# Transposes that write pairs of tokens, and weight words whose top bits are joined by 16-bit operations

## The chip, the cores and the metric

The kernel runs on one core of a Trainium2 chip. The metric is the device time of one execution in microseconds. The core has five engines that work from queues of their own: TensorE (PE in the profile, with its weight loads as PEld), VectorE (DVE), ScalarE (ACT), GpSimd (POOL) and SyncE (SP), which here only issues DMAs. Each engine takes its instructions in order, and an instruction that waits holds up all those behind it on its engine.

## The reference, cut to what matters

```python
# attention: B=4, H=8, S=768, D=48
f = 1 / (1 + exp(-f_logit))
for t in range(S):
    state = f[:, :, t, :, None] * state + einsum('bhd,bhe->bhde', k[:, :, t], v[:, :, t])
    y[:, :, t] = einsum('bhd,bhde->bhe', q[:, :, t], state)
x = y.transpose(0, 2, 1, 3).reshape(3072, 384)
# feed-forward: w_gate, w_val 384 x 1536, w_out 1536 x 384
g = x @ w_gate
out = (g * (1 / (1 + exp(-g))) * (x @ w_val)) @ w_out
```

The state decays by a gate f for each token and dimension, so the attention is a linear recurrence; its result goes through a gated feed-forward block. The activations are float32. The weights are float64: setup multiplies float32 noise by a float64 factor, and the kernel gets each weight as two 32-bit words.

## The kernel before, in words

**Units.** The tokens of a sequence are cut into six chunks of 128 (`c` from 0 to 5). A unit is one chunk of one of the four batches; unit `u` is `4 * c + b`. Within a unit, products of the gates along the tokens (two scans on VectorE) turn the recurrence into matrix products: k is multiplied by the product of the gates behind it up to the chunk's end, q by the product up to it over that of the whole chunk, scores are `k` times `q` under a causal mask, and the state of the chunk before comes in as one more product. The generator `attention(u)` yields after each step, so that the caller can lay the steps among other work.

**Getting tokens onto the free axis.** f, k and q come with tokens on partitions, and the scans need tokens along the free axis. For chunks 0 and 1 TensorE transposes them (`transposed`). For chunks 2 to 5 (`c >= SQUARES`) VectorE does, in blocks of 32 by 32. To make this work, `load` puts token `4 * t + i` of a unit on partition `t` of a group of 32, in four runs `i`, into one "room" each for f, k and q (tiles `fsquares`, `ksquares`, `qsquares`; one buffer each). A transpose of run `i` then gives every fourth token, and `in_turn` writes them to every fourth word of a row of 128 tokens.

**The steps of a unit of chunks 2 to 5,** with their lines: sigmoid of f on ScalarE (L556), transpose of f (L565), transpose of k into `kT` (L572), scan `tail` (L576), multiply of kT by it in place (L584); for units 14 to 19 (`turned`) a transpose of kT into the tile `qT`, used as scratch, and DMAs that write it to DRAM (L591, L594), from where it is read back as `kt` (L627); scan `gate` (L598), transpose of q into `qT` (L601), multiply of qT by the gate in place (L604); scores on TensorE (L617), mask on VectorE (L631), products `y` (L652, L656, L677), copies of them on ScalarE (`yT`, L660) and ten DMAs `xT<-yT` on SyncE (L667) that put them in place for the feed-forward. The last batch of a chunk takes another way to `xT`: GpSimd clears a tile `diagonal` (L544), ScalarE fills it (L546), and `y` is one set of products (L677). `yT` and `diagonal` share one buffer (tag "x").

**Loading ahead.** `load_after(u)` issues the DMAs of the next unit's f, k and q, four each, on SyncE. In chunks 2 to 5 it stands right behind L601. Since each room has one buffer, the f load waits for the end of L565, the k load for L572 and the q load for L601.

**The feed-forward** of a chunk takes all four batches at once (512 tokens). Chunk 0 is done plainly. Chunks 1 to 5 use a scheme with fifteen products in place of eighteen for the first two matrices (L957) and seven in place of eight for the third (`down_seven`: `one`, `six`, `two`, `three`, `four`, `five`, `seven`; L1056 and L1119). It costs VectorE and ScalarE additions and copies of the parts (L858, L861, L909, L962, L973). `two` ends with a copy on ScalarE of the bank "B" (L1082), of which there is one; `four` writes that bank next.

**Weights.** Each piece is fetched with its two words interleaved. ScalarE makes `up`, the low word times 2^-29 rounded to an integer, and `top`, the absolute value of the high word read as float32 (L461, L463: `sizes`). VectorE then clamps `top` (L469), shifts it left by three (L471), puts the top two bits of the high word above it (L473) and adds `up` as integers (L475): `join`. The last is named CUSTOM_DVE in the profile.

**Order.** For the start (up to about 45 us) and again from about 135 us on the order on each engine is written out: `in_order` ties every instruction to the one before it. In the latter stretch the order comes from a table of due times (`CHAINS`, `SCORES`, `times`), by which the steps of the units are laid among the products of the feed-forward. In between, while chunk 1's attention, chunk 0's feed-forward, the weights and the weights' sums run, instructions are tied only in part, and the order is the framework's.

Of the kernel before, what the change touches and what calls it, by code (L numbers as in the profile page):

```python
# [9 lines left out]
FP32 = mybir.dt.float32  # L10
I32 = mybir.dt.int32
U32 = mybir.dt.uint32
AF = mybir.ActivationFunctionType
ALU = mybir.AluOpType

# [4 lines left out]
def general_path(ctx, tc, q, k, v, f_logit, moe_w_gate, moe_w_val, moe_w_out, out):  # L20
# [70 lines left out]
    def weight_pieces(dst, src):  # L91
# [9 lines left out]
        def piece(i, j):  # L101
# [13 lines left out]
            nc.vector.tensor_scalar(man, top, 2.0 ** -20, 1.0, op0=ALU.mult, op1=ALU.add)  # L115
            nc.vector.scalar_tensor_tensor(man, lo.bitcast(U32), 2.0 ** -52, man, op0=ALU.mult, op1=ALU.add)
            nc.gpsimd.tensor_tensor(dst[:, i:i + n_a, j:j + n_n], man, p2.bitcast(FP32), ALU.mult)
# [14 lines left out]
    def attention(u):  # L132
        b, c = units[u]
        fr, qr, kr = (raw[nm][u % NRAW] for nm in "fqk")
        nc.scalar.activation(fr[:, :, 0:D], fr[:, :, 0:D], AF.Sigmoid)

# [108 lines left out]
    def mlp(g):  # L245
        h = {}

        def hidden(j):
# [5 lines left out]
            sg = ffn.tile([128, TB], FP32, tag="silu", name="silu", bufs=3)  # L254
            nc.scalar.activation(sg, gp, AF.Silu)
            h[j] = ffn.tile([128, TB], FP32, tag="h", name="h", bufs=16)
# [33 lines left out]
def short_path(ctx, tc, ident, least, judge, q, k, v, f_logit, moe_w_gate, moe_w_val, moe_w_out, out):  # L290
# [9 lines left out]
    nc = tc.nc  # L300
    B, H, S, D = q.shape
    C = 128
    NCH = S // C
    HP = H // 2
# [6 lines left out]
    N1 = C + 1  # L311
# [3 lines left out]
    SQUARES = 2  # L315
# [47 lines left out]
    def pairs(t, off=0):  # L363
        return t[:, off:off + HP * N1].rearrange("p (a t) -> p a t", t=N1)
# [30 lines left out]
    NI = C // Q  # L395
    RUN = NI * D

    rooms = {}
# [9 lines left out]
    def squares(nm):  # L408
        return rooms[nm][:, Q:Q + HP * RUN].rearrange("t (a i e) -> t a i e", a=HP, i=NI)[:, :, :, 0:Q]

    def in_turn(t):

        return t.rearrange("p a (t i) -> p a i t", i=NI)

    def load(u, what="fkqv"):
        b, c = units[u]
        rows = slice(c * C, (c + 1) * C)
        for nm, src in (("f", f_logit), ("k", k), ("q", q), ("v", v)):
            if nm not in what:
                continue  # L420
            if nm == "v":
                dst = v_of(u)
            elif c < SQUARES:
                dst = raw[nm][u % NRAW]
            else:
                for n in range(4):
                    at = Q * (1 - n % 2)
                    nc.sync.dma_start(
                        out=rooms[nm][Q * n:Q * (n + 1), at:at + HP * RUN].rearrange("t (a e) -> t a e", a=HP),
                        in_=src[b, n // 2::2, rows, :].rearrange("a (t i) d -> t a (i d)", i=NI))  # L430
                continue
            nc.sync.dma_start(out=dst[:, :, 0:D], in_=src[b, :, rows, :].rearrange("h t d -> t h d"))

    def weight_piece(dst, src, parts):

        b, a, n = dst.shape[1:]  # L440
        if src.dtype == FP32:
            by_row = src.rearrange("p a (b n) -> p a b n", n=n)
            return (lambda: [nc.sync.dma_start(out=dst[:, :, i], in_=by_row[:, i]) for i in range(a)]), [], []
        shape = [128, b // parts, a, n]
        kept = {}

        def fetch():
            kept["w"] = wst.tile([128, a, 2 * b * n], I32, tag="w64", name="w64", bufs=4)
            nc.sync.dma_start(out=kept["w"], in_=src)

        def part(m):
            return slice(m * b // parts, (m + 1) * b // parts)

        def halves(m):
            words = kept["w"].rearrange("p a (b n two) -> p a b n two", two=2, n=n)[:, :, part(m)].rearrange("p a b n two -> p b a n two")
            return words[:, :, :, :, 0], words[:, :, :, :, 1]

        def sizes(m):
            lo, hi = halves(m)
            up = wst.tile(shape, I32, tag="up", name="up", bufs=NPART)  # L460
            nc.scalar.activation(up, lo.bitcast(U32), AF.Copy, scale=2.0 ** -29)  # L461
            top = wst.tile(shape, I32, tag="top", name="top", bufs=NPART)
            nc.scalar.activation(top.bitcast(FP32), hi.bitcast(FP32), AF.Abs)  # L463
            kept["up", m], kept["top", m] = up, top

        def join(m):
            lo, hi = halves(m)
            up, top = kept["up", m], kept["top", m]
            nc.vector.tensor_scalar(top.bitcast(FP32), top.bitcast(FP32), as_float(0x38000000), as_float(0x47F00000),  # L469
                                    op0=ALU.max, op1=ALU.min)  # L470
            nc.vector.tensor_scalar(top, top, 3, 0x3FFFFFFF, op0=ALU.logical_shift_left, op1=ALU.bitwise_and)  # L471
            for i in range(b // parts):
                nc.vector.scalar_tensor_tensor(top[:, i], hi[:, i], -(1 << 30), top[:, i], op0=ALU.bitwise_and,  # L473
                                               op1=ALU.bitwise_or)
            nc.vector.tensor_tensor(dst[:, part(m)].bitcast(I32), top, up, ALU.add)  # L475

        return fetch, [lambda m=m: sizes(m) for m in range(parts)], [lambda m=m: join(m) for m in range(parts)]

    def as_float(bits):
        return struct.unpack("<f", struct.pack("<I", bits))[0]  # L480
# [31 lines left out]
    def rows_of(par):  # L512
        return slice(W * par, W * par + D)
# [3 lines left out]
    def bank(name):  # L517
        return banks[-1].tile([128, 512], FP32, tag="a", name=name)
# [3 lines left out]
    def sigmoid_ahead(u):  # L522


        fr = raw["f"][u % NRAW]
        nc.scalar.activation(fr, fr, AF.Sigmoid)
        ahead.add(u)

    def attention(u):
        b, c = units[u]  # L530
        fr, kr, qr = (raw[nm][u % NRAW] for nm in "fkq")
        v_ = v_of(u)
        gate, tail = (x[u % NROT if c < SQUARES else 0] for x in (gates, tails))

        diagonal = None

        def decay():
            nonlocal diagonal
            if c:
                nc.vector.tensor_tensor(decayed[:, :, 0:D], states[b], whole.broadcast_to((128, HP, D)), ALU.mult)  # L540
            if c and b == B - 1:

                diagonal = att.tile([128, HP, 2 * D], FP32, tag="x", name="diagonal")
                nc.gpsimd.memset(diagonal, 0.0)  # L544
                for par in range(2):
                    nc.scalar.copy(diagonal[rows_of(par), :, par * D:(par + 1) * D], decayed[rows_of(par), :, 0:D])  # L546

        def transposed(name, src):
            p = bank(name)
            for a in range(HP):  # L550
                nc.tensor.transpose(p[:, a * C:(a + 1) * C],
                                    src[:, 2 * a:2 * a + 2, :].rearrange("t r d -> t (r d)"), ident)
            return p.rearrange("p (a t) -> p a t", t=C)

        if c >= SQUARES:
            nc.scalar.activation(squares("f"), squares("f"), AF.Sigmoid)  # L556
            if b == (c > SQUARES):

                nc.scalar.activation(spare, spare, AF.Silu)
        else:  # L560
            p = transposed("fTp", fr)
# [6 lines left out]
        kT = att.tile([128, HP, C], FP32, tag="kT", name="kT")  # L568
        qT = att.tile([128, HP, C], FP32, tag="qT", name="qT", bufs=2)
        kp, qp = kT, qT  # L570
        if c >= SQUARES:
            nc.vector.transpose(in_turn(kT), squares("k"))  # L572
        yield

        n = HP * N1
        nc.vector.tensor_tensor_scan(tail[:, 0:n][:, ::-1], gate[:, 0:n][:, ::-1], floor[:, ::-1], 1.0,  # L576
                                     op0=ALU.mult, op1=ALU.max)
# [3 lines left out]
        if c < SQUARES:  # L581
            kp = transposed("kTp", kr)
            qp = transposed("qTp", qr)
        nc.vector.tensor_tensor(kT, kp, pairs(tail, 2)[:, :, 0:C], ALU.mult)  # L584
        yield
        turned = (SQUARES + 1) * B + 1 < u < (NCH - 1) * B
        if turned:
# [10 lines left out]
        nc.vector.tensor_tensor_scan(gate[:, 0:n], gate[:, 0:n], start, 1.0, op0=ALU.mult, op1=ALU.add)  # L598
        yield
        if c >= SQUARES:  # L600
            nc.vector.transpose(in_turn(qT), squares("q"))  # L601
            load_after(u)
        yield
        nc.vector.tensor_tensor(qT, qp, pairs(gate)[:, :, 1:N1], ALU.mult)  # L604
        nc.gpsimd.memset(pairs(gate)[:, :, 0:1], 0.0)
        if 0 < c < SQUARES:
            load_after(u)
        if c < SQUARES:
            decay()
# [8 lines left out]
        if c < NCH - 1 and not turned:  # L618
            p = bank("kt")
# [14 lines left out]
        if c >= SQUARES:  # L634
            decay()
# [4 lines left out]
        if c and b < B - 1:  # L640
# [20 lines left out]
            for h in range(H):  # L661
                a, par = h // 2, h % 2
                f = h * D
                while f < (h + 1) * D:
                    n = min((h + 1) * D, (f // 128 + 1) * 128) - f
# [28 lines left out]
        if c < NCH - 1:  # L694
            p = bank("dS")
# [13 lines left out]
    def load_after(u):  # L709

        w = u + (1 if units[u][1] >= SQUARES else 2)
        if w < len(units) and (units[w][1] >= SQUARES) == (w == u + 1):
            load(w, "fkqv" if units[w][1] < SQUARES or w == SQUARES * B else "fkq")
# [452 lines left out]
    mark = traced[-1]  # L1166
    keep_warm(5)
    first = [attention(b) for b in range(B)]
    done = [0] * B

# [119 lines left out]
def kernel(  # L1290
# [22 lines left out]
    def judge(bank):  # L1313
# [12 lines left out]
        yield  # L1326

    short_path(tc, ident, least, judge, *args)
    with tc.If(redo[0] > 0):
        general_path(tc, *args)  # L1330
# [32 lines left out]
```

## Time and profile before

| | us |
|---|---|
| median of three runs | 610.28 (609.24 to 611.36) |
| the profiled execution | 611.44 |
| its span, first to last instruction | 609.6 |
| TensorE busy | 595.8 |
| VectorE busy | 494.3 |
| ScalarE busy | 288.5 |
| GpSimd busy | 7.6 |

Busy time is the union of an engine's own instructions; issuing DMAs is not counted. A line of a group reads: line, engine, operation, output and inputs by name, shape, number of instructions, then their busy time, the mean time of one in ns, and the time that the engine stood idle right before them with what ended it. A line of a timeline reads: start, duration, engine, line, operation, names, shape, count, and idle time before. SPq and ACTq are DMA issues. The profile covers one execution, 1.16 us slower than the median. TensorE was granted full clock for 99.6% of the span.

### The profile page before, as it was taken

Reading aid. Unit: us, or ns where it says so; the run is one execution under the profiler, and the core shown is the slowest. Engines: PE = TensorE matmul, PEld = TensorE weight load, DVE = VectorE, ACT = ScalarE, POOL = GpSimd, SP = SyncE. Lnnn points to the kernel's source line nnn. Section 1 sums busy time; section 2 is a strip of 40 time slices with the busy share of each in tenths; the row PEclk is TensorE's granted clock in tenths of the full one; section 3 lists DMA queues with packets and bytes.
Section 4 is the critical chain, followed back from the end, with each engine's and each line's share of the span. In section 5 each row is a group of like instructions: output and inputs, shape, how many; then the busy total and the mean of one; then the engine's idle time right before and its main releaser. Section 6 shows DMA issues by size and latency. Waiting matters only on the chain.

```text
span 609.6 us, 10796 instructions
## 1 busy us (share of the span) xinstructions
PE 595.8 (98%) x4036; PEld 491.1 (81%) x4036; DVE 494.3 (81%) x833; ACT 288.5 (47%) x554; POOL 7.6 (1%) x52
## 2 busy tenths in 40 slices
PE   7899999999999999999999999999999999999996
PEld 5744545667888799888899988899988899988896
DVE  7999989868999985999996789996878981566731
ACT  3466644313776522476732366742276730366600
POOL 1000000000000000000000000000000000000000
PEclk9999999999999999999999999999999999999999
DMA  9988372005312044323236334145313100100001
GB/s 199 260 194 295 126 247 79 5 15 159 95 39 70 23 108 115 105 53 96 61 89 145 94 97 110 35 112 120 110 44 90 27 6 10 53 1 1 0 1 59
DMA packets 109142, 54.10 MB, mean 89 GB/s; under 512 B 68760, under 2 KB 102168, under 8 KB 109080
## 3 DMA queue, kind: packets, MB, share of 16 engines
q1 hardware_dynamic: 107064, 50.56, 31.3%
q10 hardware_dynamic: 2016, 2.75, 1.2%
q8 instruction: 34, 0.56, 0.4%
q14 instruction: 28, 0.23, 0.1%
HBM read 44.04 MB, written 6.29 MB: 83 GB/s over the span
## 4 chain that ended last, share of the span: by engine, by line
PE 85%; DVE 10%; SPq 1%; issue 1%; DMA 1%; ACT 1%; POOL 0%; DVEq 0%; ACTq 0%; POOLq 0%
PE o L1056 17%; PE A L957 15%; PE B L957 12%; PE gate L755 5%; PE val L755 5%; PE o L957 5%; PE c L957 5%; PE sc L617 4%; PE o L778 3%; PE o L1119 3%; PE y L677 2%; PE y L656 2%; PE dS L697 2%; PE y L652 1%; DVE c L861 1%
## 5 line engine op out<-in xcount | busy, mean ns | idle before, releaser
L1056 PE MATMUL o<-w_out,h 128*128 128x192 f32 x360 | 62.0, 327 | 0.5 <-DVE h L909 0.5
L957 PE MATMUL A<-xs,w_both 128*128 128x256 f32 x240 | 62.1, 381 | 0.0
L1056 PEld LDWEIGHTS o<-w_out,h 128*128 128x128 f32 x360 | 58.7, 190 | 1.7 <-DVE h L909 0.8
L962 ACT COPY c<-A 128x512 f32<-128x512 f32 x40 | 23.3, 583 | 62.6 <-PE A L957 62.6
L962 ACT COPY aside<-A 128x512 f32<-128x512 f32 x60 | 35.1, 584 | 32.6 <-PE A L957 32.6
L858 DVE TENSOR_TENSOR c<-c,aside 128x512 f32<-128x512 f32 x60 | 41.6, 694 | 10.5 <-ACT aside L962 9.0
L957 PEld LDWEIGHTS A<-xs,w_both 128*128 128x128 f32 x240 | 44.9, 190 | 6.5
L909 DVE TENSOR_TENSOR h<-h,c 128x256 f32<-128x256 f32 x100 | 41.1, 419 | 7.3 <-ACT h L973 7.3
L861 DVE TENSOR_TENSOR c<-c,aside 128x512 f32<-128x512 f32 x60 | 41.4, 689 | 2.5 <-ACT aside L962 2.5
L973 ACT ACTIVATE h<-c 128x256 f32<-128x256 f32 x100 | 39.2, 416 | 8.4 <-DVE c L858 5.8
L1056 PE MATMUL o<-ws,h 128*128 128x192 f32 x240 | 41.5, 328 | 0.2 <-DVE A L631 0.2
L957 PE MATMUL B<-xs,w_both 128*128 128x256 f32 x160 | 41.2, 380 | 0.6 <-ACT aside L962 0.6
L957 PE MATMUL c<-xT,w_both 128*128 128x256 f32 x160 | 41.2, 380 | 0.5 <-DVE c L861 0.5
L957 PE MATMUL A<-xs,extra 128*128 128x256 f32 x160 | 41.2, 380 | 0.0
L957 PE MATMUL B<-xT,extra 128*128 128x256 f32 x160 | 41.1, 379 | 0.0
L962 ACT COPY aside<-B 128x512 f32<-128x512 f32 x60 | 35.1, 584 | 11.7 <-PE B L957 7.2
L631 DVE TENSOR_TENSOR A<-sc,causal 128x512 f32<-128x512 f32 x48 | 30.8, 684 | 11.3 <-PE sc L617 11.3
L1056 PEld LDWEIGHTS o<-ws,h 128*128 128x128 f32 x240 | 39.1, 190 | 0.8 <-DVE A L631 0.4
L861 DVE TENSOR_TENSOR c<-o,c 128x512 f32<-128x512 f32 x40 | 27.6, 690 | 10.0 <-ACT h L973 5.8
L957 PEld LDWEIGHTS c<-xT,w_both 128*128 128x128 f32 x160 | 30.3, 190 | 5.0 <-DVE c L861 0.9
L957 PEld LDWEIGHTS B<-xs,w_both 128*128 128x128 f32 x160 | 30.2, 190 | 5.0 <-ACT aside L962 1.0
L957 PEld LDWEIGHTS A<-xs,extra 128*128 128x128 f32 x160 | 30.3, 190 | 4.5 <-ACT c L962 0.4
(138 smaller groups left out, 1140.2 us busy)
## 6 DMA issues: line engine op xcount, KB each, us to landing
fsquares<-in_f_logit_dram SPq DMA_DIRECT2D x64, 96.0 KB, 2.6
ksquares<-in_k_dram SPq DMA_DIRECT2D x64, 96.0 KB, 2.3
qsquares<-in_q_dram SPq DMA_DIRECT2D x64, 96.0 KB, 2.2
v<-in_v_dram SPq DMA_DIRECT2D x24, 192.0 KB, 3.0
w<-in_moe_w_gate_dram SPq DMA_DIRECT2D x6, 768.0 KB, 6.3
w<-in_moe_w_val_dram SPq DMA_DIRECT2D x6, 768.0 KB, 5.1
w<-in_moe_w_out_dram SPq DMA_DIRECT2D x6, 768.0 KB, 5.3
out_dram<-ob ACTq DMA_DIRECT2D x14, 192.0 KB, 2.7
```

The lines of the kernel that those rows point to most:

```text
L617: nc.tensor.matmul(sc[par][:, a * C:(a + 1) * C], lhsT=kT[r, a, :], rhs=qT[r, a, :], start=True, stop=True)
L631: nc.vector.tensor_tensor(A[:, par], sc[par].rearrange("p (a t) -> p a t", t=C), causal.unsqueeze(1).broadcast_to((128, HP, C)), ALU.mult)
L755: nc.tensor.matmul(p, lhsT=w[:, j, i, :], rhs=xT[c][:, i, :], start=(i == 0), stop=(i == KT - 1))
L778: nc.tensor.matmul(p, lhsT=hidden_tile(h, n // 2)[:, n % 2 * 2 + b // 2, b % 2 * C:(b % 2 + 1) * C], rhs=w_out[:, j, :], start=(n == 0), s ...
L858: nc.vector.tensor_tensor(dst, a, b, ALU.add)
L861: nc.vector.tensor_tensor(dst, a, b, ALU.subtract)
L909: lagging.append(lambda: f(*args))
L957: nc.tensor.matmul(p[name][:, n, :], lhsT=weights_of[a][:, n, j, :], rhs=tokens[b], start=fresh and n == 0, stop=True, skip_group_check=True)
L962: nc.scalar.copy(t, p[name])
L973: nc.scalar.activation(dst, src[:, 0, :], AF.Silu)
L1056: nc.tensor.matmul(p[:, n, :], lhsT=lhsTs[j][:, n * C:(n + 1) * C], rhs=rhs[:, j, :], start=first and j == order[0] and n == 0, stop=j == ...
L1119: nc.tensor.matmul(p, lhsT=hidden_tile(h, j)[:, 2, n * C:(n + 1) * C], rhs=b22[:, j, :], start=j == order[0], stop=j == order[-1])
```

## The change

Two edits go together.

In the weights, ScalarE writes the rounded low word only into the lower 16 bits of each word of `up`. VectorE masks the topmost 16 bits of the high word with 0xC000 and writes them into the upper 16 bits of `up`, one instruction for a join. The instructions L473 (one, or two, for a join) are gone, and the sum of `top` and `up` is as before.

In chunks 2 to 5, the transposes of k and q write two runs of tokens to every second word of one half of a row, and the other two runs to the other half (`parted`). The multiplies that follow read such a row in pairs of words, two from one half and two from the other, and write tokens in their right order (`multiply`). The two transposes therefore write scratch tiles and no longer the tiles that are multiplied in place: k goes to the tile `qT`, and q to k's room. `load_after` moves behind the multiply of q, since k's room is in use until then. The transpose of f is as before.

```diff
+        def split_squares(nm):
+            return squares(nm).rearrange("t a (j i) e -> t a j i e", j=2)
+        def parted(t):
+            return t.rearrange("p (j a t i) -> p a j i t", j=2, a=HP, i=NI // 2)
...
+        def high_ends(m):
+            quarters = kept["w"].bitcast(U16).rearrange("p a (b n four) -> p a b n four", four=4, n=n)[:, :, part(m)]
+            return quarters.rearrange("p a b n four -> p b a n four")[:, :, :, :, 3]
...
-            nc.scalar.activation(up, lo.bitcast(U32), AF.Copy, scale=2.0 ** -29)
+            ends = up.bitcast(U16).rearrange("p b a (n two) -> p b a n two", two=2)
+            nc.scalar.activation(ends[:, :, :, :, 0], lo.bitcast(U32), AF.Copy, scale=2.0 ** -29)
...
-            for i in range(b // parts):
-                nc.vector.scalar_tensor_tensor(top[:, i], hi[:, i], -(1 << 30), top[:, i], op0=ALU.bitwise_and,
-                                               op1=ALU.bitwise_or)
+            ends = up.bitcast(U16).rearrange("p b a (n two) -> p b a n two", two=2)
+            nc.vector.tensor_single_scalar(ends[:, :, :, :, 1], high_ends(m), 0xC000, op=ALU.bitwise_and)
             nc.vector.tensor_tensor(dst[:, part(m)].bitcast(I32), top, up, ALU.add)
...
+        def multiply(out, x, by):
+            if c >= SQUARES:
+                for_each = "p a (t j i) -> p a t j i"
+                out, by = (t.rearrange(for_each, j=2, i=NI // 2) for t in (out, by))
+                x = x.rearrange("p (j a t i) -> p a t j i", j=2, a=HP, i=NI // 2)
+            nc.vector.tensor_tensor(out, x, by, ALU.mult)
...
         if c >= SQUARES:
-            nc.vector.transpose(in_turn(kT), squares("k"))
+            kp = qT.rearrange("p a t -> p (a t)")
+            nc.vector.transpose(parted(kp), split_squares("k"))
...
-        nc.vector.tensor_tensor(kT, kp, pairs(tail, 2)[:, :, 0:C], ALU.mult)
+        multiply(kT, kp, pairs(tail, 2)[:, :, 0:C])
...
         if c >= SQUARES:
-            nc.vector.transpose(in_turn(qT), squares("q"))
-            load_after(u)
+            qp = rooms["k"][:, 0:HP * C]
+            nc.vector.transpose(parted(qp), split_squares("q"))
         yield
-        nc.vector.tensor_tensor(qT, qp, pairs(gate)[:, :, 1:N1], ALU.mult)
+        multiply(qT, qp, pairs(gate)[:, :, 1:N1])
         nc.gpsimd.memset(pairs(gate)[:, :, 0:1], 0.0)
-        if 0 < c < SQUARES:
+        if c:
             load_after(u)
```

More of the change, by code (lines that the diff above doesn't have):

```diff
@@ L12 @@
 U32 = mybir.dt.uint32
+U16 = mybir.dt.uint16
 AF = mybir.ActivationFunctionType
```

## The prediction

> **What bounds the kernel now.** I read the page's busy shares first, then the waits, then busy time by stretch, then the groups, then the timelines of single queues. The page:
>
> ```profile
> PE 595.8 (98%) x4036; PEld 491.1 (81%) x4036; DVE 494.3 (81%) x833; ACT 288.5 (47%) x554; POOL 7.6 (1%) x52
> ```
>
> What TensorE waited for (total us, times, longest us):
>
> ```profile
> PE sc L617 <- DVE qT L604: 2.5, 3, 1.0
> ...
> PE B L957 <- ACT aside L962: 0.6, 1, 0.6
> PE o L1056 <- DVE h L909: 0.5, 1, 0.5
> PE c L957 <- DVE c L861: 0.5, 1, 0.5
> ```
>
> TensorE is busy for 595.8 of 609.6 us, so 13.8 us is all that any faster VectorE could return. By stretches, 3.3 us of it lies in the first 15 us (start-up) and 5.8 us behind the last matmul; neither touches the change. That leaves 2.1 us between 15 and 50 us, 0.8 between 100 and 150, and 2.2 in all the rest, of which one stretch holds most:
>
> ```profile
> 170.00:190.00 20.00, 20.00 (x144) 17.00 (x142) 18.86 (x32) 14.58 (x29) 0.10 (x1) 1.00 0.31 80
> 190.00:210.00 20.00, 18.46 (x88) 15.52 (x88) 19.48 (x34) 10.13 (x22) 0.11 (x1) 1.00 0.08 20
> ```
>
> (Columns: stretch, length, busy PE, PEld, DVE, ACT, POOL.) From 190 to 210 us, in the fifteen-product part of the feed-forward for chunk 1, VectorE is full (19.48 of 20) and TensorE idles for 1.54 us, in the last three of the waits above.
>
> [...] a step of four words: 1113 ns for 512 columns against 702 ns for a dense destination. [...] The trace shows that in L469, 551 ns for 768 elements where the two-source L473 takes 956.
>
> **Part 1, the words of the weights.** Groups by line, shapes kept apart:
>
> ```profile
> L473 DVE SCALAR_TENSOR_TENSOR top<-w,top 128x384 int32<-128x384 int32 x24 | 12.6, 554 | 0.4
> L469 DVE TENSOR_SCALAR top<-top 128x768 f32<-128x768 f32 x16 | 8.8, 551 | 3.0 <-ACT top L463 2.8
> L473 DVE SCALAR_TENSOR_TENSOR top<-w,top 128x768 int32<-128x768 int32 x6 | 5.7, 956 | 0.1
> ```
>
> Thirty L473 (18.3 us) go; twenty one-source 16-bit operations come, 16 of 768 elements and 4 of 384. At L469's price they cost 16 x 0.551 + 4 x 0.352 = 10.2 us, so VectorE is relieved of 8.1 us; [...] 16 x 0.956 + 4 x 0.554 = 17.5, relief 0.8. I take the former. ScalarE's L461 writes as many elements, only narrower: I take its 922 ns as they are [...]. Between 50 and 100 us TensorE is busy for 50.00 of 50.00 us, so relief there is worth nothing. It can pay twice. At 27.90 us the products `y` take 1.91 instead of 1.10 us because the mask L631 comes behind a join, which gets shorter by 0.20 (0.56 to 0.35). At 126.5 us `sc` waits 0.78 us for L604, and L473 at 124.20 (0.95) is two instructions ahead of it: 0.40. Sum **-0.6 us** (bounds 0 and -1.0).
>
> **Part 2, the transposes.**
>
> ```profile
> L601 DVE STREAM_TRANSPOSE qT<-qsquares 128x512 f32<-128x512 f32 x16 | 18.0, 1125 | 6.4 <-DMA turn<-qT 6.4
> L572 DVE STREAM_TRANSPOSE kT<-ksquares 128x512 f32<-128x512 f32 x16 | 17.8, 1113 | 0.0
> L591 DVE STREAM_TRANSPOSE qT<-kT 128x512 f32<-128x512 f32 x6 | 4.2, 702 | 0.0
> ```
>
> L601 and L572 write every fourth word, L591 dense words. The new ones write every second word; bounds 702 and 1113, I take 702: 32 x 0.41 = 13 us less on VectorE. The 32 multiplies L584 and L604 then read pairs of words with a hop between pairs[...]: 0 taken [...].
>
> What of the 13 us reaches TensorE: in 190 to 210 us VectorE works without a gap from 178.6 on. L572 at 182.62 is 0.41 shorter, so the wait of 0.56 at 192.46 falls to 0.15; with L601 at 195.65 also shorter, VectorE is 0.82 ahead, TensorE 0.41, and the wait of 0.48 at 199.25 falls to 0.07; the one of 0.50 at 208.8 then keeps its size. Gain 0.82. Further, L601's 6.4 us of waiting for `turn<-qT` goes, since q is no longer transposed into the tile that the DMA still reads; L604 now waits there, about 2 us later in VectorE's order. At 355.57 us `sc` took 1.66 instead of 1.16 us behind such a late L604: 0.5. Sum **-1.3 us** (bounds 0 and -2.0). That k's transpose writes qT earlier costs nothing: the last reader two units back has always ended (closest: reads of qT by `y` that end at 290.2 and 329.7 us against k's transposes at 294.0 and 333.5).
>
> **What is moved, and past what.** `load_after` issues 12 DMAs on SyncE (four each for f, k, q) and moves from L601's step to L604's. f still waits only for its own transpose. k's room is now scratch until L604 ends, so k, and q behind it in the queue, start after L604. They need 1.74 + 1.74 us of issue, and everything later in the queue slips. In unit 12 the load also moves past a v load, so f comes 4 us later (landed about 243): ScalarE, 4.8 us idle before 245.83, covers it. Transposes of the next k come 4 us or more after the L604 in question, against 3.6 us from issue to landing, but for unit 17, where VectorE idles anyway. Two places have no cover. The first, in order of queues SP, POOL, ACT, PE:
>
> ```profile
> 310.55 1.74 SPq L428 DMA_DIRECT2D qsquares<-in_q_dram  x4
> 313.55 6.81 SPq L667 DMA_DIRECT2D xT<-yT  x10
> ...
> 321.66 0.42 POOL L544 MEMSET diagonal<- 128x384 f32 x1 [8.53 <-DMA xT<-yT]
> ...
> 322.11 0.71 ACT L546 COPY diagonal<-decayed 48x192 f32<-48x192 f32 x2 [8.05 <-POOL diagonal L544]
> 322.84 0.48 ACT L1082 COPY ob<-o 128x384 f32<-128x384 f32 x1
> ...
> 324.87 4.06 PE L1056 MATMUL o<-ws,hs 128*128 128x192 f32 x24
> ```
>
> L604 of unit 15 ends at 312.9 (about 312.5 after). k and q issue until about 316.2, so the ten `xT<-yT` run from 316.3 to 322.5, 2.2 us later than now. POOL clears the tile that they read, ScalarE fills it, and behind that in ScalarE's order stands L1082, which empties the only bank "B" before the product `four` at 324.87. L1082 ended at 323.32, slack 1.55; it slips by 2.2: TensorE waits 0.6 us. At the end of the next chunk, L604 of unit 19 ends at 406.9, the ten issues start at about 410.3 instead of 407.5, L1082 ends at 419.8 instead of 417.0, and `four` at 418.85 waits 0.95 us. At the end of chunk 2 the f load keeps SyncE busy until 223.0, past L604's end at 222.1: no slip. Sum **+1.55 us** (bounds 0 and +5). The later f of units 17 and 21 makes ScalarE's sigmoids 2 us later; VectorE and ScalarE idle there for 1.2 us or more right after.
>
> **Sum.** -0.6 - 1.3 + 1.55 = -0.35 us. The profiled execution took 611.44 us (span 609.6), 1.16 above the median of 610.28; I apply the sum to the median: **609.9 us**. A measurement of this kernel can tell about 0.3%, 1.8 us: no change.
>
> **Rivals.**
> 1. The transfers are early enough and nothing slips: all of the gain stays. -1.9 us gives 608.4, with the upper bounds 607.3. For it: L601's waits vanish, so L604 and the loads may come earlier than I put them. Against: nothing in the listed idle time allows over 3 us after the start-up.
> 2. Slower: SyncE's queue. One mechanism: k and q wait for L604, the `xT<-yT` behind them slip by S, and TensorE loses S - 1.55 and S - 1.85 us before the two products `four`. It decides from S of about 3.5: with S = 4 (issues in this trace took 2.5 to 4.3 us for four [...], f at 324.41 3.59) the loss is 4.6 us, and 610.28 - 1.9 + 4.6 = 613.0.
> 3. It doesn't do what it says: a step of two words costs like one of four [...]. Then only the slip is left: 610.28 + 1.55 + up to 0.5 = 612.0.
> 4. From 50 to 135 us the order is not written by hand: the trace shows the steps of a join (112.54, 117.15, 118.74, 124.20) among the sums of the weights. Other instructions can be ordered otherwise; worth up to 0.8 us down, 1 to 3 us up.
>
> **Chances.** My forecast 0.45; rival 1 0.20; rivals 2, 3 and 4 0.18, 0.10 and 0.07. Faster by over 0.3% comes from rival 1's better part and a little of my own spread: 0.20. Slower comes from 2, most of 3 and 4, and the upper end of mine: 0.35. Same: 0.45. The range from 607.9 to 613.2 leaves 2 in 10 outside; my own case alone is 608.6 to 611.4.
>
> **What would show it.** Right: L572 and L601 near 0.7 us, multiplies still 0.69, TensorE's idle time in 190 to 210 us near 0.7, k's loads starting with the end of L604, `xT<-yT` near 316 and 410 us, and waits of 0.5 to 1 us of `o` L1056 for ScalarE's L1082 in these two places. Wrong: no such waits (rival 1), waits of over 2 us (rival 2), transposes still at 1.1 us (rival 3), or a different order of TensorE between 50 and 135 us with new idle time (rival 4).

## The result and the profile after

The changed kernel takes 611.58 us (median of 22 runs, 610.95 to 613.66), the kernel before 610.33 us (median of 22 runs on the same chip). The ratio of the two is estimated at 1.0027, 95% interval 1.0018 to 1.0036: 1.65 us slower, give or take 0.55 (the bare medians differ by 1.25). The forecast was 609.9 us, 0.35 faster, with a range up to 613.2. The time lies in the range, on the other side of no change, about 2 us from the forecast. In the batches further down, a run of 770.74 and one of 880.01 us had a granted clock of 0.753 and 0.656 and are left out of the ratios. The profiled execution of the changed kernel took 613.66 us, the slowest of its runs, with a span of 611.8 us.

The line of busy shares, from the page of the kernel after:

```profile
PE 594.2 (97%) x4036; PEld 489.1 (80%) x4036; DVE 475.3 (78%) x823; ACT 290.6 (47%) x554; POOL 7.8 (1%) x52
```

VectorE is relieved of 19.0 us (494.3 to 475.3), close to the 21 that the sizes of the parts promised. TensorE does the same work in a longer span. The groups by line of the kernel after, shapes kept apart (busy us, mean ns | idle before):

```profile
L595 DVE STREAM_TRANSPOSE qT<-ksquares 128x512 f32<-128x512 f32 x16 | 11.3, 705 | 0.7 <-DMA ksquares<-in_k_dram 0.6
L625 DVE STREAM_TRANSPOSE ksquares<-qsquares 128x512 f32<-128x512 f32 x16 | 11.1, 696 | 0.0
L557 DVE TENSOR_TENSOR qT<-ksquares,gates 128x512 f32<-128x512 f32 x16 | 10.9, 684 | 5.5 <-DMA turn<-qT 5.5
...
L488 DVE TENSOR_SCALAR up<-w 128x768 uint16<-128x768 uint16 x16 | 9.7, 606 | 0.8 <-DMA w<-in_moe_w_val_dram 0.7
L614 DVE STREAM_TRANSPOSE qT<-kT 128x512 f32<-128x512 f32 x6 | 4.2, 702 | 0.0
...
L488 DVE TENSOR_SCALAR up<-w 128x384 uint16<-128x384 uint16 x4 | 2.3, 586 | 0.0
```

The transposes that write pairs run as fast as the dense one of L614, and the multiplies behind them have their old price (684 ns for q and 673 for k, against 696 and 674 in the kernel before). The transposes take 13.4 us less in all (35.8 to 22.4), as forecast; the weights' instructions 6.3 us less (18.3 to 12.0), where 8.1 were forecast. Now the waits of TensorE, kernel after (total us, times, longest):

```profile
PE o L1079 <- ACT ob L1105: 2.8, 2, 1.5
PE sc L640 <- DVE qT L557: 2.5, 3, 1.5
...
PE y L700 <- ACT diagonal L568: 0.6, 1, 0.6
PE o L1079 <- DVE h L932: 0.5, 1, 0.5
...
PE B L980 <- ACT c L985: 0.4, 1, 0.4
```

The first line is new: twice the product `four` (L1079, L1056 before) waits for ScalarE's copy of bank B (L1105, L1082 before). Busy time by stretch shows where it lies (stretch, length, busy PE, PEld, DVE, ACT, POOL):

```profile
190.00:210.00 20.00, 19.05 (x130) 16.18 (x132) 19.45 (x33) 11.77 (x25) 0.10 (x1) 1.00 0.15 40
...
300.00:350.00 50.00, 48.03 (x383) 44.40 (x382) 38.35 (x67) 15.36 (x33) 0.63 (x3) 1.00 0.40 104
...
400.00:450.00 50.00, 48.76 (x411) 44.98 (x409) 38.21 (x66) 17.16 (x34) 0.73 (x4) 1.00 0.33 91
```

In 190 to 210 us TensorE idles for 0.95 us in place of 1.54. In 300 to 350 and in 400 to 450 it idles for 1.97 and 1.24 us, where it was busy without a gap before. The two places are the ends of chunks 3 and 4. Their timelines in the kernel after, queues in the order SP, POOL, ACT, PE, DVE:

```profile
310.35 1.74 SPq L438 DMA_DIRECT2D ksquares<-in_k_dram  x4
312.13 2.89 SPq L438 DMA_DIRECT2D qsquares<-in_q_dram  x4
315.12 6.26 SPq L690 DMA_DIRECT2D xT<-yT  x10
...
325.44 3.77 SPq L438 DMA_DIRECT2D fsquares<-in_f_logit_dram  x4
...
406.15 1.74 SPq L438 DMA_DIRECT2D ksquares<-in_k_dram  x4
407.94 1.86 SPq L438 DMA_DIRECT2D qsquares<-in_q_dram  x4
409.90 6.73 SPq L690 DMA_DIRECT2D xT<-yT  x10
...
322.68 0.42 POOL L566 MEMSET diagonal<- 128x384 f32 x1 [12.13 <-DMA xT<-yT]
...
323.13 0.71 ACT L568 COPY diagonal<-decayed 48x192 f32<-48x192 f32 x2 [11.25 <-POOL diagonal L566]
323.86 0.48 ACT L1105 COPY ob<-o 128x384 f32<-128x384 f32 x1
332.87 0.63 ACT L578 ACTIVATE fsquares<-fsquares 128x512 f32<-128x512 f32 x1 [8.52 <-DMA fsquares<-in_f_logit_dram]
...
324.39 4.17 PE L1079 MATMUL o<-ws,hs 128*128 128x192 f32 x24 [1.54 <-ACT ob L1105]
...
343.81 1.13 PE L980 MATMUL B<-xT,extra 128*128 128x256 f32 x4 [0.42 <-ACT c L985]
...
419.90 4.17 PE L1079 MATMUL o<-ws,hs 128*128 128x192 f32 x24 [1.25 <-ACT ob L1105]
...
333.59 1.11 DVE L587 STREAM_TRANSPOSE gates<-fsquares 128x512 f32<-128x512 f32 x1 [2.89 <-ACT fsquares L578]
```

k, q and the ten `xT<-yT` stand in one row on SyncE. The clearing on POOL follows the last of them, the fill and L1105 follow on ScalarE, and `four` follows L1105: the chain that the prediction names.

**Marks.** To place gains and losses I take the starts of the score products (`sc`) of units 0 to 23. A unit's distance to an earlier one, minus the same distance in the kernel before, is what that stretch lost (positive) or gained, in us of one profiled execution each:

| kernel | 4 to 6 | 6 to 7 | 9 to 10 | 10 to 12 | 15 to 16 | 16 to 17 | 17 to 18 | 19 to 20 | 4 to 23 | ratio of the timed runs |
|---|---|---|---|---|---|---|---|---|---|---|
| after | 0.02 | -0.51 | -0.54 | 0.30 | 1.81 | 0.51 | -0.50 | 1.51 | 2.61 | 1.0027 |
| w_only | 0.12 | -0.50 | 0.20 | -0.10 | 0.00 | 0.07 | 0.00 | 0.00 | -0.21 | 0.9999 |
| t_only | 0.00 | 0.00 | -0.71 | -0.58 | 1.78 | 0.18 | -0.50 | 1.37 | 1.54 | 1.0045 |
| move_only | 0.18 | -0.01 | 0.08 | 0.44 | 2.22 | -0.18 | -0.50 | 1.88 | 4.11 | 1.0095 |
| slip4 | 1.47 | 0.00 | -0.02 | -0.36 | 0.79 | -0.18 | -0.50 | 0.00 | 1.21 | 1.0041 |
| slip9 | 1.11 | -0.01 | 0.04 | -0.62 | 2.58 | -0.17 | -0.44 | 2.25 | 4.74 | 1.0140 |
| fill_late | 0.00 | -0.50 | -0.54 | 0.05 | 1.58 | 0.27 | -0.50 | 0.00 | 0.36 | 1.0015 |
| fill_late_unturned | 0.50 | -0.50 | -0.54 | -0.73 | 0.66 | 0.22 | -0.50 | 0.00 | -0.89 | 0.9995 |
| before_fill_late | 0.00 | 0.00 | 0.04 | 0.35 | 0.00 | -0.17 | -0.02 | 0.00 | 0.20 | 1.0001 |
| tail_scratch | 0.44 | -0.50 | -0.63 | -0.73 | 0.00 | -0.18 | -0.50 | 0.00 | -2.19 | 0.9979 |
| tail_scratch_t_only | 0.00 | 0.00 | -0.79 | -0.22 | 0.00 | -0.18 | -0.50 | 0.00 | -1.78 | 0.9983 |
| tail_scratch_fill_late | 0.00 | -0.51 | -0.62 | -0.29 | 0.00 | -0.18 | -0.50 | 0.00 | -2.20 | 0.9966 |

Stretches after unit 4 that are left out differ by 0.1 us or less. The column 10 to 12 goes from -0.73 to 0.44 and has -0.62 in slip9, whose edit does nothing there; no gain or loss is read from it. The stretch up to unit 4 is left out of the sums because the profiled execution of the kernel before lost time there that is not the kernel's own. Busy time by stretch of the kernel before, with the granted clock as the third number from the end:

```profile
28.00:31.40 3.40, 3.40 (x49) 2.79 (x49) 3.23 (x8) 1.75 (x5) 0.00 (x0) 0.50 0.78 256
```

For 3.4 us TensorE had half its clock, and unit 4 starts 1.46 us later than in the kernel after. (The 99.6% given for the kernel before is this mean of the granted clock, 0.996 over the span.) The profile of before_fill_late shows such a dip too: its granted clock from 15 to 50 us is 0.95, as in the kernel before. Those of the kernel after, w_only, t_only, fill_late and the three tail_scratch kernels have 1.00 there. The kernels w_only and before take the same time in the timed runs though only one of their profiles has the dip, so I put no gain down to it.

### The profile page after: what moved, and what is told of

It is laid out like the page before. It is cut to its first block, busy times and chain, and to the rows that moved or that the text cites. A ratio compares the mean times of both kernels' runs of the same rounds, so it can differ in the third digit from the quotient of the medians.

```text
span 611.8 us, 10782 instructions
## 1 busy us (share of the span) xinstructions
PE 594.2 (97%) x4036; PEld 489.1 (80%) x4036; DVE 475.3 (78%) x823; ACT 290.6 (47%) x554; POOL 7.8 (1%) x52
## 4 chain that ended last, share of the span: by engine, by line
PE 76%; DVE 12%; SPq 6%; issue 2%; ACT 1%; DMA 1%; POOL 0%; DVEq 0%; ACTq 0%; POOLq 0%
PE A L980 15%; PE B L980 13%; PE o L1079 10%; PE c L980 5%; PE gate L778 5%; PE o L980 5%; PE val L778 5%; PE sc L640 3%; PE o L801 3%; SPq L690 3%; SPq L438 3%; PE o L1142 3%; PE y L700 2%; PE y L679 2%; PE dS L720 1%
## 5 line engine op out<-in xcount | busy, mean ns | idle before, releaser
L1079 PE MATMUL o<-w_out,h 128*128 128x192 f32 x360 | 62.0, 328 | 0.5 <-DVE h L932 0.5
L1079 PEld LDWEIGHTS o<-w_out,h 128*128 128x128 f32 x360 | 58.7, 190 | 1.7 <-DVE h L932 0.8
L985 ACT COPY aside<-A 128x512 f32<-128x512 f32 x60 | 35.1, 585 | 33.1 <-PE A L980 33.1
L985 ACT COPY c<-A 128x512 f32<-128x512 f32 x40 | 23.3, 582 | 54.2 <-PE A L980 48.8
L1079 PE MATMUL o<-ws,h 128*128 128x192 f32 x240 | 41.5, 328 | 0.2 <-DVE A L654 0.2
L985 ACT COPY aside<-B 128x512 f32<-128x512 f32 x60 | 35.1, 584 | 9.9 <-PE B L980 7.7
L1079 PEld LDWEIGHTS o<-ws,h 128*128 128x128 f32 x240 | 39.1, 190 | 0.8 <-DVE A L654 0.4
L980 PEld LDWEIGHTS B<-xT,extra 128*128 128x128 f32 x160 | 30.2, 190 | 5.0 <-ACT c L985 0.8
L881 DVE TENSOR_TENSOR c<-c,o 128x384 f32<-128x384 f32 x15 | 8.3, 550 | 33.1 <-PE o L1079 33.1
```

Source lines behind the costliest of these rows:

```text
L881: nc.vector.tensor_tensor(dst, a, b, ALU.add)
L980: nc.tensor.matmul(p[name][:, n, :], lhsT=weights_of[a][:, n, j, :], rhs=tokens[b], start=fresh and n == 0, stop=True, skip_group_check=True)
L985: nc.scalar.copy(t, p[name])
L1079: nc.tensor.matmul(p[:, n, :], lhsT=lhsTs[j][:, n * C:(n + 1) * C], rhs=rhs[:, j, :], start=first and j == order[0] and n == 0, stop=j == ...
```

## The experiments

Ratios are to the kernel before, which ran beside each batch (medians 609.66, 609.94 and 609.93 us).

**w_only: the weights' edit alone.** The kernel before, with this in place of L461 and L473:

```diff
-            nc.scalar.activation(up, lo.bitcast(U32), AF.Copy, scale=2.0 ** -29)
+            nc.scalar.activation(ends[:, :, :, :, 0], lo.bitcast(U32), AF.Copy, scale=2.0 ** -29)
...
-            for i in range(b // parts):
-                nc.vector.scalar_tensor_tensor(top[:, i], hi[:, i], -(1 << 30), top[:, i], ...)
+            nc.vector.tensor_single_scalar(ends[:, :, :, :, 1], high_ends(m), 0xC000, op=ALU.bitwise_and)
```

> The weights' words alone, on the kernel before. Queue theory (the loss comes from k's and q's loads that slip behind L604): this part is a small gain, 0.5 us faster than before (ratio 0.999), TensorE's wait at about 125 us down from 0.78 to 0.3, the one-source operation 0.6 us each. Rival (the loss comes from the weights: ScalarE's conversions to 16 bits take 0.15 us longer each and the order between 50 and 135 us is another): 1.5 us slower than before (ratio 1.0025), with new idle time of TensorE before 135 us.

Measured: 609.93 us, ratio 0.9999 (0.9989 to 1.0009). In the marks the sums' stretch before unit 7 gains 0.50 us, which is the wait of `sc` at 126.5 us that the prediction named (0.78 us before, 0.27 here), and 0.32 is lost again in 4 to 6 and 9 to 10. What is left, 0.21 us, is less than these runs can tell. The rival's 1.0025 lies outside the interval.

**t_only: the transposes and the move of the loads alone.** The kernel after with the two weight edits undone.

> The transposes, the scratch tiles and the moved loads alone, on the kernel before. Queue theory: gains of 1.2 us between 190 and 380 us, losses of 3.5 us at the ends of chunks 3 and 4 and at their follow-ups, so 2.2 us slower than before (ratio 1.0036); two waits of TensorE for L1105's counterpart of 1.2 to 1.6 us. Rival (the loss comes from the weights): 1 us faster than before.

Measured: 612.16 us, ratio 1.0045 (1.0032 to 1.0058). The losses at the ends of chunks 3 and 4 (1.78 and 1.37 us) come with this part. Why the time is above the 1.0027 of the full change by more than the weights' edit gains alone is open; the two intervals overlap.

**move_only: the new places of q's transpose and of the loads, without faster transposes.** The kernel before with:

```diff
-            nc.vector.transpose(in_turn(qT), squares("q"))
-            load_after(u)
+            qp = rooms["k"][:, 0:HP * C].rearrange("p (a t) -> p a t", a=HP)
+            nc.vector.transpose(in_turn(qp), squares("q"))
...
-        if 0 < c < SQUARES:
+        if c:
             load_after(u)
```

> The kernel before with only the move: k as before, q transposed in the old steps of four words into k's room, multiplied from there into qT, and the loads behind the multiply. No operation of VectorE gets shorter, and none gets a new step. Queue theory: k's and q's loads start 0.4 us later than in the changed kernel, the two waits for the copy of bank B come to 3.2 us, the turn's wait of 0.5 us goes, together about 3 us slower than before (ratio 1.005). Rival (what costs is the pairwise reading and the two-word step on VectorE): as before, within 0.3%.

Measured: 615.6 us, ratio 1.0095 (1.0073 to 1.0118), more than expected. Timeline of move_only, SP and PE:

```profile
314.02 2.90 SPq L428 DMA_DIRECT2D qsquares<-in_q_dram  x4
317.03 6.27 SPq L667 DMA_DIRECT2D xT<-yT  x10
...
326.31 4.17 PE L1056 MATMUL o<-ws,hs 128*128 128x192 f32 x24 [1.95 <-ACT ob L1082]
...
421.48 4.17 PE L1056 MATMUL o<-ws,hs 128*128 128x192 f32 x24 [1.61 <-ACT ob L1082]
```

The move makes both waits by itself, with every transpose at its old price. q again takes 2.90 us to issue right behind k. The two ends of chunks cost 4.1 us in the marks; what makes the rest of the 5.8 us is open.

**slip4 and slip9: the slip alone.** The kernel before, with 4 or 9 small DMAs on SyncE that nothing reads, ahead of the ten `xT<-yT` of chunks 3 and 4. No tile and no load of the kernel is touched:

```diff
+            if u in (14, 18):
+                idle = att.tile([128, 16], FP32, tag=f"idle{u}", name="idle")
+                for i in range(4):
+                    nc.sync.dma_start(out=idle[:, i:i + 1], in_=f_logit[0, 0, 0:128, i:i + 1])
```

> The kernel before with four tiny loads of their own on SyncE ahead of the ten xT<-yT of units 14 and 18 and nothing else changed. Queue theory: they delay these by about 0.5 and 1.2 us, less than the slack of 1.55 and 1.85 us of the copy of bank B: no change, within 0.2%. Rival (every us by which SyncE is late costs one, without a slack): 1.7 us slower.

> As with four, but nine tiny loads. Queue theory: delay of about 2.7 and 3.4 us; loss at the end of chunk 3 about 1.2 to 1.8 us, at the end of chunk 4 about 1.5, together 3 us slower (ratio 1.005), with TensorE's waits for the copy L1082 of bank B. Rival (SyncE's lateness is not the cause in the changed kernel): no change.

Measured: slip4 612.89 us, ratio 1.0041 (1.0028 to 1.0054), where I had expected none; slip9 618.01 us, ratio 1.0140 (1.0119 to 1.0161), more than expected. Timeline of slip4, SP, DVE and PE:

```profile
313.21 1.85 SPq L664 DMA_DIRECT2D idle<-in_f_logit_dram  x4
315.16 6.72 SPq L671 DMA_DIRECT2D xT<-yT  x10
...
330.89 1.14 DVE L601 STREAM_TRANSPOSE qT<-qsquares 128x512 f32<-128x512 f32 x1 [4.39 <-DMA fsquares<-in_f_logit_dram]
...
332.81 1.16 PE L617 MATMUL sc<-qT,kT 48*128 48x128 f32 x16 [0.72 <-DVE qT L604]
```

and of slip9:

```profile
313.02 5.13 SPq L664 DMA_DIRECT2D idle<-in_f_logit_dram  x9
318.24 6.25 SPq L671 DMA_DIRECT2D xT<-yT  x10
...
332.49 1.14 DVE L601 STREAM_TRANSPOSE qT<-qsquares 128x512 f32<-128x512 f32 x1 [6.18 <-DMA turn<-qT]
...
327.62 4.17 PE L1060 MATMUL o<-ws,hs 128*128 128x192 f32 x24 [1.91 <-ACT ob L1086]
```

In slip4 `four` doesn't wait. Set on the time of the kernel before, the copy of bank B ends 1.0 us late at the end of chunk 3 and 1.5 at the end of chunk 4, inside the slacks of 1.55 and 1.85. At the end of chunk 4 nothing is lost (0.00), against the rival. At the end of chunk 3 0.79 us is lost, in another place: the scores behind `four` wait for L604, and that stands behind L601, which writes the tile that `turn<-qT` reads; `turn<-qT` stands behind the `xT<-yT` on SyncE. This is a second limit, which the prediction did not see. The profile names `turn<-qT` as what L601 waited for in slip9, and in slip4 the f load issued right behind it. In slip9 `four` waits for 1.91 and 1.98 us. Both kernels also lose time where the edit has nothing. Up to unit 4, TensorE waits 1.0 and 2.2 us for the first loads of f. Between units 4 and 6, in the stretch whose order is the framework's, 1.1 to 1.5 us is lost, in slip4 0.93 of it as waits of the plain feed-forward's third product for `h`. The chip's runs of slip9 lose 8.5 us where the marks have 4.74. What makes these further microseconds is open. So only the places in the profile are used from these two, not their ratios.

**fill_late: what waits behind the slip is taken off ScalarE's way.** The kernel after, with the clearing and the fill of `diagonal` one step later, so that L1105 stands ahead of them in ScalarE's order:

```diff
+        if c >= SQUARES:
+            decay()
+            yield
+            fill()
...
-        return [[f, *steps, s + 0.02, s + masks[kind], s + 2.2, o, o + 0.01, o + 2.1]
+        return [[f, *steps, s + 0.02, s + masks[kind], s + 2.2, s + 4.2, o, o + 0.01, o + 2.1]
```

> Both parts as changed, but the tile diagonal is cleared and filled in a step of its own, two units of the due times later, so that it stands behind the copy of bank B in ScalarE's order. The loads still slip. Queue theory: the two waits for that copy, 2.8 us together, are gone, the time is 1.1 us below before (ratio 0.998), 2.8 us below the changed kernel. Rival (the waits are a symptom, and TensorE is late for another reason): TensorE waits as long at the next place, 1.6 us slower than before.

Measured: 610.66 us, ratio 1.0015 (1.0002 to 1.0027), where I had expected 0.998. Waits of TensorE and timeline (PE, DVE) of fill_late:

```profile
PE sc L645 <- DVE qT L557: 4.4, 4, 1.8
```

```profile
330.29 1.16 PE L645 MATMUL sc<-qT,kT 48*128 48x128 f32 x16 [1.51 <-DVE qT L557]
...
329.54 0.69 DVE L557 TENSOR_TENSOR qT<-ksquares,gates 128x512 f32<-128x512 f32 x1 [5.73 <-DMA turn<-qT]
```

No wait for `ob` is left. At the end of chunk 4 the whole loss is gone (1.51 to 0.00), which shows that it was this chain. At the end of chunk 3 the loss only changes its name: 1.58 for 1.81 us. `four` starts in time and the scores behind it wait for L557, which starts at 329.54 as it did in the kernel after. The second limit lay right under the first.

**fill_late_unturned: the second limit away as well.** fill_late, and unit 16 makes its `kt` by TensorE and not by way of DRAM (`turned = ... and u != 16`), so that L557 has no `turn<-qT` to wait for.

> The kernel fill_late (both parts changed, diagonal filled behind the copy of bank B), and unit 16 transposes kT on TensorE instead of by way of DRAM, so that its multiply of q waits for no DMA. In fill_late TensorE waited 1.51 us for that multiply at the end of chunk 3, which waited for turn<-qT behind the slipped xT<-yT. Queue theory: that wait goes, four transposes on TensorE (0.45 us) come, so 1.0 us below fill_late, about even with before. Rival (a third thing holds TensorE there): as fill_late.

Measured: 609.68 us, ratio 0.9995 (0.9984 to 1.0005). The loss at the end of chunk 3 falls from 1.58 to 0.66 us. Timeline (PE) of fill_late_unturned:

```profile
328.48 0.67 PE L727 MATMUL dS<-v,kt 128*64 128x48 f32 x16 [0.59 <-DMA kt<-turn]
```

What is left is a third transfer behind the `xT<-yT` in the same queue, the read of unit 15's `kt`. With the two larger limits gone the kernel after is as fast as before.

**before_fill_late: the control for fill_late.** The same edit in the kernel before.

> The kernel before, with the one edit of fill_late: the fill of `diagonal` stands one step later in ScalarE's order, behind the copy of bank B (L1082), at the ends of chunks 2 to 4. My theory says that L1082 has 1.55 us of slack in the kernel before, so that nothing waits for it and the edit is worth nothing: ratio 0.9990 to 1.0010, no wait of `o` for `ob` before or behind. The rival, that the later fill is worth something by itself and that fill_late's gain on the kernel after is this and not the slip, expects about 0.9985.

Measured: 610.54 us, ratio 1.0001 (0.9990 to 1.0011). The later fill is worth nothing where the queue doesn't slip.

**tail_scratch: the pairs without the move of the loads.** The kernel after, with q's transpose writing into the tile of `tail`, which is free by then, and `load_after` back in its old place; a copy of `least` that reads `tail` moves ahead:

```diff
-            qp = rooms["k"][:, 0:HP * C]
+            qp = tail[:, 0:HP * C]
             nc.vector.transpose(parted(qp), split_squares("q"))
+            load_after(u)
...
-        if c:
+        if 0 < c < SQUARES:
             load_after(u)
```

> Both parts as changed, but q is transposed into the tile of the tails, which is free from the multiply of k on when its four values at the chunk's start are copied out a few steps earlier; so k's room is no scratch, and the loads are back at q's transpose as in the kernel before. Queue theory: no slip, the gains alone stay: 1.7 us faster than before (ratio 0.997), xT<-yT right behind yT as before, no waits for the copy of bank B. Rival (the slip is not the cause): 1.6 us slower than before, like the changed kernel.

Measured: 608.36 us, ratio 0.9979 (0.9972 to 0.9987), faster than both kernels. Timeline (SP, ACT) and busy time by stretch of tail_scratch:

```profile
307.13 1.74 SPq L438 DMA_DIRECT2D qsquares<-in_q_dram  x4
310.58 7.13 SPq L695 DMA_DIRECT2D xT<-yT  x10
...
320.19 0.48 ACT L1110 COPY ob<-o 128x384 f32<-128x384 f32 x1
```

```profile
300.00:350.00 50.00, 50.00 (x393) 46.53 (x392) 40.60 (x71) 16.77 (x35) 0.73 (x4) 1.00 0.43 111
```

q's issue has ended 1.7 us before the `xT<-yT` begin, L1110 (the copy of bank B) ends 3.7 us earlier than in the kernel after, 2.9 of it against the mark of unit 15, and TensorE has no gap at either end of a chunk.

**tail_scratch_t_only and tail_scratch_fill_late.** tail_scratch with the words of the weights as before; and tail_scratch with the later fill.

> tail_scratch with the words of the weights as in the kernel before: the transposes by pairs, q's scratch in the tile of `tail`, the loads back at q's transpose. If the gain of tail_scratch (0.9979) is the transposes' once the loads don't move, the ratio is 0.9980 to 0.9986, since the weights' edit was worth 0.2 to 0.5 us in the marks of w_only and after. If the weights' edit carries part of it only together with the transposes, or the new place of the loads is what gains, 0.9990 or above.

> tail_scratch with the fill of `diagonal` one step later, as in fill_late. In tail_scratch no wait of `o` for `ob` is left, so my theory says that the later fill adds nothing: the same ratio as tail_scratch within 0.0008, 0.9972 to 0.9987. The rival: the diagonal still holds something up at the ends of chunks (ScalarE stood 8 us for it in the kernel before), and the two edits add up: 0.9965 or below.

Measured: 608.95 us, ratio 0.9983 (0.9975 to 0.9991), and 608.10 us, ratio 0.9966 (0.9954 to 0.9978). The gain of tail_scratch stays without the weights' edit, which adds at most some tenths; what carries it is the transposes with the loads in their old place. The earlier copy of `least` is in all three kernels and was not tried alone. The later fill on top leaves the marks where they were (2.20 and 2.19 us). Its ratio is below the range that I had expected and next to the rival's 0.9965, but its interval overlaps that of tail_scratch, and no place in the profile goes with it. A gain is neither shown nor ruled out; it is the fastest of the kernels that ran.

## Why the prediction was wrong, step by step

**The weights (-0.6 us): sign right, smaller.** 0.51 us before unit 7 in the kernel after, 0.21 net and no measurable time in w_only. One of its two terms was a misreading: the products `y` at 27.90 us took 1.91 us in the kernel before because of the halved clock, not because of the mask behind a join; in the kernel after, at a granted clock of 1.00, they took 1.21. The window above shows the clock (0.50), which the prediction left out of account. The price also was low: 0.606 against 0.551 us for the large shape and 0.586 against 0.352 for the small one. It was L469's, as the alternative of 17.5 us was L473's; that the 16-bit operation would cost the same was my estimate, and the trace of the kernel before has no such operation.

**The transposes (-1.3 us): the price right, the gain in part.** The trace of the kernel before has no transpose that writes every second word; that it would cost what dense words cost was my estimate. It took 705 and 696 ns, against 702 for dense words in this trace and 1113 for every fourth word in the kernel before. That the multiplies would lose nothing by reading pairs with a hop between them was an estimate too, and L557 bears it out: 684 and 673 ns. Idle time in 190 to 210 us fell from 1.54 to 0.95 us, where about 0.7 was forecast. The 0.50 us at unit 17 came as forecast, but slip4, with the old transposes, has it too: there L601 started 1.1 us earlier behind `turn<-qT` (set on the mark of unit 16), and move_only, with the old transposes in their new place, has it as well. So the pairs are not shown to be its cause. Timed without the slip, in tail_scratch_t_only, this part is worth 1.0 us (0.5 to 1.5).

**"Sum +1.55 us (bounds 0 and +5)": the step that failed.** The mechanism, the place and the instruction are as forecast; the size is not. In the marks the two ends cost 1.81 + 1.51 = 3.3 us, 2.8 of them as waits for L1105. The slack of 1.55 us that the prediction read off is right. Set on the time of the kernel before (by the mark of unit 15), L1105 slipped by 3.2 us in the kernel after, by 3.57 in slip9 and by 3.61 in move_only; less 1.55 this gives 1.65, 2.02 and 2.06, and the waits are 1.54, 1.91 and 1.95. The term that was mis-sized is the slip, 2.2 us forecast at the end of chunk 3 and 3.2 measured. k started where it should (310.35, which is 312.53 on the time of the kernel before; forecast 312.5). But q was priced at 1.74 us, its price with 2.4 us of rest between k and q. Its four issues now took 2.89; one of them took 1.26 us, where the first took 0.43. At the end of chunk 4 q took 1.86 us, the start of the `xT<-yT` was met within 0.1 us, the ten issues took 6.73 us in place of 6.26, and the copy of bank B came 0.4 us later than put down. Together the two ends cost 1.75 us more than forecast, which is most of the 2 us by which the whole was off.

That q stood right behind k is not what decides its price. In the kernel after it did so at both ends, and took 2.89 us at the end of chunk 3 and 1.86 at the end of chunk 4. In move_only, fill_late and fill_late_unturned it took 2.90, 3.08 and 3.24 us at the end of chunk 3. The trace of the kernel before has both prices as well, each right behind k:

```profile
236.70 1.81 SPq L428 DMA_DIRECT2D ksquares<-in_k_dram  x4
238.61 3.06 SPq L428 DMA_DIRECT2D qsquares<-in_q_dram  x4
...
351.40 1.85 SPq L428 DMA_DIRECT2D ksquares<-in_k_dram  x4
353.35 1.80 SPq L428 DMA_DIRECT2D qsquares<-in_q_dram  x4
```

What makes an issue take longer is open. The mistake was to take one row, the lowest, for a price that ranges from 1.74 to 3.1 us in that trace.

**Two costs put at nothing.** "The later f of units 17 and 21" was said to be covered by idle VectorE and ScalarE. Set on the time of the kernel before (by the mark of unit 16) the sigmoid came 3.3 us later, not 2. VectorE waited 2.89 us for it (L587) and was then late with the copies and sums, so that TensorE waited 0.42 for L985: 0.51 us in 16 to 17. The cover was 1.2 us and more, and the slip was over twice that. t_only loses only 0.18 us there, so how much of it comes back in every run is open; no run isolates it. "At the end of chunk 2 no slip" was nearly so: the wait for `diagonal` grew from 0.29 to 0.59 us. t_only has no loss there, so this is small and not steady. The next k was not quite covered either: L595 waited 0.63 us for it (at 315.12), but VectorE was ahead by then, and L614 came at its old time.

**A limit not seen.** At the end of chunk 3 the chain through `turn<-qT`, L557 and `sc` came 0.2 us behind the one through bank B. A mended order on ScalarE alone would have returned only half.

**The rivals.** The outcome lies between my case and rival 2, the queue with a larger slip, whose reason was the right one: issues that take longer than 1.74 us. I knew such rows (2.5 to 4.3 us) and used them for the rival, not for the forecast. Rivals 1 and 3 are refuted by the waits and by the prices of the transposes; of rival 4, a new order between 50 and 135 us, the kernel after shows 0.02 us in 4 to 6.

The sum of the marks, 2.6 us, is above the 1.65 (1.1 to 2.2) of the timed runs; for t_only, move_only, slip4 and slip9 it is below, by 1.2 to 3.8 us. One profiled execution of each is not good to better than about 1 us here, and worse for the slower kernels.

## What to carry to other kernels

Price a DMA issue by the range of its rows in the trace, and carry the range through the slack: here four issues took 2.9 us where 1.7 was put down, and TensorE waited 1.54 us behind them in place of 0.6. A scratch tile costs the transfers that would otherwise fill it: with q's scratch in one tile the change was 1.65 us slower, in another 1.3 us faster (0.0021 of 610 us), and what differs at the places of the loss is what the loads had to wait for. Before counting on a stall being mended, look for the next wait right behind it, and check the granted clock before you explain a long product.

## What the runs showed of the hardware

- A transpose of 512 columns that writes every second word takes 705 ns, as one that writes dense words (702), where every fourth word takes 1113.
- The 16-bit one-source operation (L488) took 606 ns for 768 elements and 586 for 384: 0.8 and 1.5 ns an element. The smaller shape costs about what the two-source L473 of that size did (554).
- ScalarE's copy into 16-bit halves of 32-bit words (L476) took 1082 ns for 768 elements, where the 32-bit one (L461) took 922.
- Four issues of the same size on SyncE took from 1.74 us (q in the kernel before, at 310.55) to 4.61 (f in fill_late, at 325.67). Neither a rest before them nor other issues right ahead tells which: in the kernel before, q took 1.74 us after 2.4 us of rest (310.55), 2.51 after 2.7 (404.52), and 1.80 to 3.06 right behind k.
- On ScalarE L1105 (the copy of bank B), which stands behind the fill L568, started at 323.86, 0.02 us after the fill, which had waited 11.25 us. With the fill behind that copy (fill_late) `four` started at 322.43, ahead of the fill (323.05).
- TensorE's granted clock was 0.50 for 3.4 us (28.00 to 31.40) in the profile of the kernel before, and unit 4 started 1.46 us later than in the kernel after. Ahead of it TensorE had waited 0.79 us for L604 and 0.74 for the copy `kt`. The kernel after waited the same 0.79 us, and t_only 0.7 for `kt`, without a dip; what brings it on is open.
